# A windowed-attention kernel on one core: transposes in pairs, attention-value beside scores, other places for the convolution, an earlier patch load

## The chip, the core and the metric

The kernel runs on one core of a Trainium2 chip. The time is device time in microseconds (us). "Span" is the time from the first to the last instruction of a profiled execution. TensorE's clock is granted in two steps here, full and half (the 558 clock records of the trace before hold only 1.0 and 0.5), and "clock 0.78" is its mean. Each of these records lasts a multiple of 3.41 us; such a stretch of 3.41 us is called a window. A slot or window is called warm at full clock and cold at half.

## The reference, cut to what matters

```python
# x: (1, 511, 511, 192) bf16; windows of 7 x 7; 4 heads of 48
pe = sum(xp[:, i:i+H, j:j+W, :] * dw_pe[i, j] for i in 0..2 for j in 0..2)   # depthwise 3 x 3
x0 = x + pe
h  = layernorm(x0)                          # over the 192 channels
q, k, v = split(windows(h) @ w_qkv)         # 5329 windows of 49 positions
out = softmax(q @ k.T * 48**-0.5) @ v       # per window and head
return x0 + unwindow(out @ w_o)
```

## The kernel before: the parts that matter

A block is up to 128 windows, one on each partition, and a slot is 8 windows of it: 42 blocks, 667 slots. While the slots of block b do attention, TensorE also does block b+1's convolution (192 small matmuls, slots 0 to 7 of 16), VectorE its statistics (slots 7 to 13), GpSimd its normalisation, and TensorE again its transposes (slots 10 to 15). XP holds the patches that the convolution reads, T its matrix, X the sums x + pe and their normalised form, HO the transposed halves (later also the attention output), and pO a projection that has been copied out. To evict is to copy a result out of PSUM, where the matmuls' results (the tiles ps) lie. Three PSUM tiles of two banks each go round (`PS.next()`), so a stage can start only when the tile used three stages ago has been read.

One transposed group, eight positions, two halves of 96 channels:

```python
def ln_tr(b, s0, n):
    ps = PS.next(); pb = ps[:].bitcast(BF)
    for kt in range(2):
        for i in range(N):                       # 8 transposes into bank kt
            mm(pb[0:KT, kt*1024 + i*128 : ...], lhsT=h[:, s0+i, kt*KT:(kt+1)*KT], rhs=ident[:], is_transpose=True)
        eng = nc.vector.tensor_copy if kt == 0 else nc.scalar.copy
        eng(out=HO[b % 2][0:KT, kt, :, s0:s0+N], in_=pb[0:KT, kt*1024 : ...])
```

One slot, in the order of issue (`hook` issues portions of statistics, loads and stores; `fill` issues the convolutions that are due):

```python
stage_A(b, ck, 0, fill)          # q: 4 matmuls of 392 columns, copied by ScalarE
stage_E(...)                     # attention output transposed back, copied to HO
stage_A(b, ck, 1, fill)          # k
stage_D()                        # attention-value; VectorE: reciprocal, multiply
for s0 in pj: proj(b - 1, s0, fill)   # 8 projection matmuls; ScalarE evicts to pO, GpSimd adds
n.transpose(...)                 # ln_tr, at most one group
stage_B()                        # scores; ScalarE: exp
stage_V(b, ck, fill, ...)        # v: 8 matmuls of 192 columns
```

D and B use TensorE as four tiles of 64 x 64, all else uses the whole array.

## Time and profile before

| | before |
|---|---|
| time, median of 2 | 5380.8 us |
| profiled span | 5361.9 us |
| granted clock | 0.777 |
| before the first slot | 171.1 us |
| mean block (1 to 40) | 124.5 us |

The page lists the busy time of each engine; the list of waits gives, for each row, who waited for whom, the microseconds in total, how often, and the longest one. The prediction below shows the lines. How to read them: TensorE at 83% is not at its limit, as 592 of its some 930 us of idle time are a single wait, and part of its busy time was spent at half clock (0.777 in the mean).

### The profile page before, as it was taken

The page shows a single profiled execution, that of the slowest core. Times are in us where ns is not written, and L with a number is a line of the kernel's source. Part 1 is how long each engine was busy: PE and PEld are TensorE (multiplying, and loading weights), DVE is VectorE, ACT ScalarE, POOL GpSimd, SP SyncE. Part 2 cuts the span into 40 slices and gives each one's busy share as a digit, 9 for nine tenths or more (in the row PEclk, how much of TensorE's full clock was granted, in tenths as well). Part 3 has the DMA queues.
Part 4 walks back from the last instruction along what each step waited for, and adds up shares of the span by engine and source line. Part 5 has one row for each costly group of instructions (what it writes and reads, how often), then busy time and mean ns, then how long its engine had stood idle before and what let it go on. Part 6 is the DMA issues. An engine that isn't in the chain of part 4 may idle for free. (4 is left out here: it accounts for less than half of the span.)

```text
span 5361.9 us, 167300 instructions
## 1 busy us (share of the span) xinstructions
PE 4426.2 (83%) x75049; PEld 3610.8 (67%) x75049; DVE 2727.6 (51%) x4190; ACT 3054.3 (57%) x3855; POOL 2116.4 (39%) x1188
## 2 busy tenths in 40 slices
PE   2688888888888888888888888888888888888777
PEld 1566776776766666677766766666667776676665
DVE  5554555455555544555545555545554555455542
ACT  1455555556555565556655555555555566555555
POOL 3433333334444433334433444433333343344333
PEclk9886787777777776778877777767777888777777
DMA  2222222233333222222323333222222233233221
GB/s 69 59 68 67 68 68 68 68 78 77 82 80 83 72 68 68 68 68 68 78 68 77 83 80 83 71 67 68 68 68 68 68 78 73 70 74 81 68 48 32
DMA packets 529706, 377.00 MB, mean 70 GB/s; under 512 B 454181, under 2 KB 454373, under 8 KB 528979
## 3 DMA queue, kind: packets, MB, share of 16 engines
q1 hardware_dynamic: 528531, 365.92, 27.9%
q8 instruction: 589, 9.65, 0.8%
q14 instruction: 138, 1.13, 0.1%
q10 hardware_dynamic: 448, 0.30, 0.0%
HBM read 265.31 MB, written 100.27 MB: 68 GB/s over the span
## 5 line engine op out<-in xcount | busy, mean ns | idle before, releaser
L467 POOL TENSOR_TENSOR X<-X,pO 128x768 bf16<-128x768 bf16 (+1 forms) x546 | 894.6, 1654 | 2789.2 <-ACT pO L463 2787.9
L364 PE MATMUL ps<-HO,Wqk 96*128 96x392 bf16 x5336 | 1639.4, 426 | 20.1 <-ACT HO L352 15.8
L298 PEld LDWEIGHTS <-XP 81*128 81x128 bf16 x8064 | 1246.8, 185 | 139.2 <-issue 51.6
L298 PE MATMUL psc<-T,XP 81*128 81x49 bf16 x8064 | 1303.1, 211 | 41.3 <-DMA xs<-in_x_dram 32.0
L380 PE MATMUL ps<-Wv,HO 96*128 96x192 bf16 x5336 | 863.4, 299 | 118.3 <-DVE o L433 112.2
L343 PE MATMUL ps<-ident,X 128*96 128x128 bf16 x4116 | 412.0, 253 | 640.9 <-DVE HO L352 592.0
L432 DVE RECIPROCAL rs<-ps 128x16 f32<-128x16 f32 x667 | 169.8, 255 | 1393.8 <-PE ps L423 896.8
L303 DVE CAST X<-psc 128x490 bf16<-128x490 f32 x840 | 542.8, 646 | 591.5 <-PE psc L298 585.0
L364 PEld LDWEIGHTS <-Wqk 96*128 96x128 bf16 x5336 | 623.7, 124 | 303.8 <-issue 238.1
L352 ACT COPY HO<-ps 96x1024 bf16<-96x1024 bf16 (+1 forms) x294 | 284.5, 968 | 869.7 <-PE ps L343 869.7
L343 PEld LDWEIGHTS <-X 128*96 128x96 bf16 x4116 | 336.8, 148 | 644.7 <-issue 598.6
L372 ACT CAST k<-ps 128x784 bf16<-128x784 f32 x667 | 543.6, 815 | 363.8 <-PE ps L364 269.6
L329 POOL TENSOR_TENSOR X<-X,rstd 128x1536 bf16<-128x1536 bf16 (+1 forms) x294 | 734.2, 2515 | 18.5 <-DMA out_dram<-X 5.4
L380 PEld LDWEIGHTS <-HO 96*128 96x128 bf16 x5336 | 604.6, 122 | 158.6 <-issue 111.7
L459 PE MATMUL ps<-Wo,HO 96*128 96x192 bf16 x4116 | 690.6, 302 | 16.3 <-ACT HO L448 12.7
L388 ACT CAST v<-ps 128x768 bf16<-128x768 f32 x667 | 535.7, 803 | 267.3 <-PE ps L380 218.7
L372 ACT CAST q<-ps 128x784 bf16<-128x784 f32 x667 | 543.7, 815 | 249.2 <-PE ps L364 240.9
L433 DVE TENSOR_TENSOR o<-ps,rs 128x768 bf16<-128x768 f32 x667 | 638.4, 957 | 23.4
L459 PEld LDWEIGHTS <-HO 96*128 96x128 bf16 x4116 | 619.1, 180 | 25.2 <-issue 3.5
L463 ACT CAST pO<-ps 128x768 bf16<-128x768 f32 x504 | 401.4, 799 | 392.3 <-PE ps L459 333.4
L447 PEld LDWEIGHTS <-o 128*96 128x96 bf16 x5336 | 526.4, 166 | 104.5 <-issue 45.8
L410 ACT ACTIVATE pt<-ps 128x784 bf16<-128x784 f32 x667 | 550.8, 826 | 62.6 <-PE ps L402 62.5
(55 smaller groups left out, 4068.3 us busy)
## 6 DMA issues: line engine op xcount, KB each, us to landing
XP<-in_x_dram SPq DMA_DIRECT2D x568, 216.0 KB
xs<-in_x_dram SPq DMA_DIRECT2D x574, 168.0 KB
out_dram<-X SPq DMA_DIRECT2D x246, 336.0 KB
XP<-in_x_dram SPq DMA_DIRECT2D x151, 212.6 KB
out_dram<-X SPq DMA_DIRECT2D x82, 168.0 KB
XP<-in_x_dram SPq DMA_DIRECT2D x16, 192.0 KB
XP<-in_x_dram SPq DMA_DIRECT2D x64, 30.4 KB
xs<-in_x_dram SPq DMA_DIRECT2D x63, 23.6 KB
```

The costliest lines, as they stand in the source:

```text
L298: mm(cv.ps[:, (c % 10) * S : (c % 10 + 1) * S], lhsT=XP[0:KP, :, c], rhs=T[0:KP, c, :], start=True, stop=True)
L303: nc.vector.tensor_copy(out=self.X[cv.b % 3][:, :, c0 : c0 + n], in_=cv.ps[:, 0 : n * S].rearrange("p (c s) -> p s c", s=S))
L329: nc.gpsimd.tensor_tensor(out=hbuf(b)[:, s0:s1, :], in0=self.X[b % 3][:, s0:s1, :], in1=rstd[:, i : i + n].unsqueeze(2).to_broadcast([128, ...
L343: mm(pb[0:KT, kt * 1024 + i * 128 : kt * 1024 + (i + 1) * 128], lhsT=h[:, s0 + i, kt * KT : (kt + 1) * KT], rhs=ident[:], start=True, stop ...
L364: mm(ps[:, ab * 512 : ab * 512 + TOK], lhsT=self.Wqk[kt][0:KT, which * 2 + ab, :], rhs=HO[b % 2][0:KT, kt, ck * CH : (ck + 1) * CH, 0:S], ...
L372: nc.scalar.copy(out=dst[:, :, 0:TOK], in_=two_bank(ps, TOK))
L380: mm(ps[:, col : col + C], lhsT=HO[b % 2][0:KT, kt, w : w + 2, :].rearrange("p w s -> p (w s)"), rhs=self.Wv[kt][0:KT, :], start=(kt == 0) ...
L388: eng(out=v_[:].rearrange("p (b j) h e -> p b (j h) e", b=2)[:, :, :, 0:DH], in_=two_bank(ps, 2 * C).rearrange("p b (g d) -> p b g d", d=DH),)
L410: nc.scalar.activation(out=pt[:, 0 : 16 * S].rearrange("p (b n) -> p b n", b=2), in_=two_bank(ps, 8 * S), func=ACTF.Exp, scale=SCALE)
L433: nc.vector.tensor_tensor(out=o_[:].rearrange("p b q (h d) -> p b (q h) d", d=DH), in0=ov[:, :, :, 0:DH], in1=r_[:].rearrange("p (b g) -> ...
L459: mm(ps[:, col : col + C], lhsT=HO[b % 2][0:KT, kt, :, s0 + i], rhs=self.Wo[kt][0:KT, :], start=(kt == 0), stop=(kt == 1))
L467: nc.gpsimd.tensor_tensor(out=xv, in0=xv, in1=o[:, 0:n, :], op=ALU.add)
```

## The change

There are four parts. (a) **Pairs**: both halves of a group are transposed before either is copied. (b) **Order**: attention-value moves behind projection and transposes, next to the scores. (c) **Places**: the convolutions go behind q and k (weight 2) and v (weight 1), no longer behind the projection. (d) **Setup**: the first patch load is issued ahead of the making of the weights, the patch buffer is cleared first and by two engines, and the convolution matrix T is evicted four positions at a time; GpSimd's clearing of X goes behind the matrix that selects for T, which is so ready earlier. The intent is to take the waits and the mode changes (between four tiles and the whole array) off TensorE: in the kernel before, at full clock, 120 ns pass from the start of the last attention-value matmul to the first of the projection (median).

```diff
 def ln_tr(...):                                  # (a)
     for kt in range(2):
         for i in range(N): mm(... is_transpose=True)
+    for kt in range(2):
         eng = nc.vector.tensor_copy if kt == 0 else nc.scalar.copy
...
-            if 0 <= g - LD < NG:                 # (b)
-                stage_D()
             for s0 in pj:
-                proj(b - 1, s0, fill)
+                proj(b - 1, s0)
...
+            if n and g < NG:
+                n.transpose(part(0.56, 0.96, 7), 0.9)
+            if 0 <= g - LD < NG:
+                stage_D()
             if g < NG:
-                if n:
-                    n.transpose(part(0.56, 0.96, 7), 0.9)
                 stage_B()
...
-            nlong = 16 + 8 * len(pj)             # (c)
-            def fill():
-                quota[0] += (conv_goal - conv_start) / nlong
+            def fill(weight):                    # 2 in stage_A, 1 in stage_V
+                quota[0] += (conv_goal - conv_start) * weight / 24
...
+        nc.vector.memset(self.XP[:, 0:88, :], 0.0)     # (d), first of all
+        nc.gpsimd.memset(self.XP[:, 88:BLK, :], 0.0)
-            for n, s0 in enumerate(range(0, S, 2)):    # T: 25 evictions
+            for n, s0 in enumerate(range(0, S, 4)):    # T: 13 evictions
+        for t in self.load_xp(0):                      # ahead of the branch, not behind it
+            t()
```

More of the change, by code (lines that the diff above doesn't have):

```diff
@@ L73, in __init__ @@
         self.PC = _Rot([psum.tile([128, 512], F32, name=f"psc{i}") for i in range(2)])
-        for t in self.PS.t + self.PC.t:
-            nc.vector.memset(t[:], 0.0)
+        self.XP = big.tile([128, BLK, C], BF, name="XP")
+        self.XPr = self.XP[0:KP].rearrange("(r q) n c -> q r n c", q=9)
+        nc.vector.memset(self.XP[:, 0:88, :], 0.0)
+        nc.gpsimd.memset(self.XP[:, 88:BLK, :], 0.0)
         self.ident = consts.tile([128, 128], BF, name="ident")
-        make_identity(nc, self.ident[:])
         self.zero = consts.tile([16, C], BF, name="zero")
         nc.vector.memset(self.zero[:], 0.0)
-        self.XP = big.tile([128, BLK, C], BF, name="XP")
-        self.XPr = self.XP[0:KP].rearrange("(r q) n c -> q r n c", q=9)
         self.T = big.tile([128, C, S], BF, name="T")
@@ L88, in __init__ @@
         gi = consts.tile([1, 1], I32, name="gi")
-        nc.vector.memset(self.XP[:], 0.0)
-        for t in self.X:
-            nc.gpsimd.memset(t[:], 0.0)
         with tc.tile_pool(name="setup", bufs=1) as setup:
@@ L97, in __init__ @@
             for j in range(3):
-                nc.sync.dma_start(out=dwK[9 * j : 9 * j + 3, :], in_=dw_pe[j])
+                nc.scalar.dma_start(out=dwK[9 * j : 9 * j + 3, :], in_=dw_pe[j])
             for kt in range(2):
@@ L115, in __init__ @@
             )
-            for n, s0 in enumerate(range(0, S, 2)):
-                ns = min(2, S - s0)
+            make_identity(nc, self.ident[:])
+            for t in self.PS.t + self.PC.t:
+                nc.vector.memset(t[:], 0.0)
+            for n, s0 in enumerate(range(0, S, 4)):
+                ns = min(4, S - s0)
                 ps = self.PS.next()
@@ L120, in __init__ @@
                     nc.tensor.matmul(
-                        ps[0:KP, ss * C : (ss + 1) * C],
+                        ps[0:KP, (ss // 2) * 512 + (ss % 2) * C : (ss // 2) * 512 + (ss % 2 + 1) * C],
                         lhsT=Sel[0:21, (s0 + ss) * KP : (s0 + ss + 1) * KP],
@@ L126, in __init__ @@
                     )
-                dst = self.T[0:KP, :, s0 : s0 + ns].rearrange("p c s -> p s c")
-                src = ps[0:KP, 0 : ns * C].rearrange("p (s c) -> p s c", c=C)
+                if ns == 4:
+                    dst = self.T[0:KP, :, s0 : s0 + ns].rearrange("p c (b s) -> p c b s", b=2)
+                    src = ps[0:KP].rearrange("p (b n) -> p b n", b=2)[:, :, 0 : 2 * C].rearrange("p b (s c) -> p c b s", c=C)
+                else:
+                    dst = self.T[0:KP, :, s0 : s0 + ns]
+                    src = ps[0:KP, 0 : ns * C].rearrange("p (s c) -> p c s", c=C)
                 (nc.vector.tensor_copy if n % 2 == 0 else nc.scalar.copy)(out=dst, in_=src)
@@ L173, in __init__ @@
             nc.vector.tensor_copy(out=gi[:], in_=gm[:])
+            for t in self.X:
+                nc.gpsimd.memset(t[:], 0.0)
+        for t in self.load_xp(0):
+            t()
         cond = nc.values_load(gi[0:1, 0:1], min_val=0, max_val=1)
@@ L181, in __init__, with dram, clear, load_xp @@
                 self.slow(c2)
+    def dram(self, t, h, w, dims):
+        return bass.AP(tensor=t.tensor, offset=t.offset + (h * self.W + w) * C, ap=[list(d) for d in dims])
+    def clear(self, part, p0, n):
+        nc, zero = self.nc, self.zero[0:9, :]
+        return lambda: nc.sync.dma_start(
+            out=part[:, p0 : p0 + n, :], in_=bass.AP(tensor=zero.tensor, offset=zero.offset, ap=[list(zero.ap[0]), [0, n], [1, C]])
+        )
+    def load_xp(self, b):
+        nc, x, XP, XPr, W, NWR, NWC = self.nc, self.x, self.XP, self.XPr, self.W, self.NWR, self.NWC
+        blocks, clear, dram = _blocks(NWR, NWC), self.clear, self.dram
+        for a0, b0, da, db, n, p0 in blocks[b]:
+            left = [0] if b0 == 0 else []
+            right = [] if b0 + (n - 1) * db < NWC - 1 else list(range(n)) if da else [n - 1]
+            if left and any(ln[1] for bb in blocks[:b] for ln in bb):
+                yield clear(XPr[0], p0, n if da else 1)
+            if right and b:
+                yield clear(XPr[8], p0 + right[0], len(right))
+            last = a0 + (n - 1) * da
+            cuts = [0] + ([1] if da and a0 == 0 else []) + ([n - 1] if da and last == NWR - 1 else []) + [n]
+            for i, j in zip(cuts, cuts[1:]):
+                if j <= i:
+                    continue
+                top, bot = a0 + i * da == 0, a0 + (j - 1) * da == NWR - 1
+                if top and b:
+                    yield clear(XP[0:9], p0 + i, j - i)
+                if bot and b:
+                    yield clear(XP[KP - 9 : KP], p0 + i, j - i)
+                pr0, pr1 = (1 if top else 0), (8 if bot else 9)
+                for pc in range(9):
+                    q, sh = (WS - 1, -1) if pc == 0 else (0, 1) if pc == 8 else (pc - 1, 0)
+                    n0, n1 = i, j
+                    if pc == 0 and left:
+                        n0 = j if da else i + 1
+                    if pc == 8 and right:
+                        n1 = i if da else j - 1
+                    if n1 <= n0:
+                        continue
+                    dims = [[W * C, pr1 - pr0], [WS * C * (W * da + db), n1 - n0], [1, C]]
+                    dst = XPr[pc, pr0:pr1, p0 + n0 : p0 + n1, :]
+                    src = dram(x, WS * (a0 + n0 * da) - 1 + pr0, WS * (b0 + n0 * db + sh) + q, dims)
+                    yield lambda dst=dst, src=src: nc.sync.dma_start(out=dst, in_=src)
@@ L221, in two_bank @@
             return ps[:].rearrange("p (b n) -> p b n", b=2)[:, :, 0:ncol]
-        def dram(t, h, w, dims):
-            return bass.AP(tensor=t.tensor, offset=t.offset + (h * W + w) * C, ap=[list(d) for d in dims])
-        zero = self.zero[0:9, :]
-        def clear(part, p0, n):
-            return lambda: nc.sync.dma_start(
-                out=part[:, p0 : p0 + n, :], in_=bass.AP(tensor=zero.tensor, offset=zero.offset, ap=[list(zero.ap[0]), [0, n], [1, C]])
-            )
-        def load_xp(b):
-            for a0, b0, da, db, n, p0 in blocks[b]:
-                left = [0] if b0 == 0 else []
-                right = [] if b0 + (n - 1) * db < NWC - 1 else list(range(n)) if da else [n - 1]
-                if left and any(ln[1] for bb in blocks[:b] for ln in bb):
-                    yield clear(XPr[0], p0, n if da else 1)
-                if right and b:
-                    yield clear(XPr[8], p0 + right[0], len(right))
-                last = a0 + (n - 1) * da
-                cuts = [0] + ([1] if da and a0 == 0 else []) + ([n - 1] if da and last == NWR - 1 else []) + [n]
-                for i, j in zip(cuts, cuts[1:]):
-                    if j <= i:
-                        continue
-                    top, bot = a0 + i * da == 0, a0 + (j - 1) * da == NWR - 1
-                    if top and b:
-                        yield clear(XP[0:9], p0 + i, j - i)
-                    if bot and b:
-                        yield clear(XP[KP - 9 : KP], p0 + i, j - i)
-                    pr0, pr1 = (1 if top else 0), (8 if bot else 9)
-                    for pc in range(9):
-                        q, sh = (WS - 1, -1) if pc == 0 else (0, 1) if pc == 8 else (pc - 1, 0)
-                        n0, n1 = i, j
-                        if pc == 0 and left:
-                            n0 = j if da else i + 1
-                        if pc == 8 and right:
-                            n1 = i if da else j - 1
-                        if n1 <= n0:
-                            continue
-                        dims = [[W * C, pr1 - pr0], [WS * C * (W * da + db), n1 - n0], [1, C]]
-                        dst = XPr[pc, pr0:pr1, p0 + n0 : p0 + n1, :]
-                        src = dram(x, WS * (a0 + n0 * da) - 1 + pr0, WS * (b0 + n0 * db + sh) + q, dims)
-                        yield lambda dst=dst, src=src: nc.sync.dma_start(out=dst, in_=src)
@@ L269, in strips @@
+        dram, load_xp = self.dram, self.load_xp
         def strips(b, r0, r1):
@@ L370, in stage_A @@
                     )
-                    fill()
+                    fill(2)
             nc.scalar.copy(out=dst[:, :, 0:TOK], in_=two_bank(ps, TOK))
@@ L386, in stage_V @@
                     )
-                    fill()
+                    fill(1)
             eng(
@@ L451, in stage_E, with proj @@
             )
-        def proj(b, s0, fill):
+        def proj(b, s0):
             n = min(4, S - s0)
@@ L459, in proj @@
                     mm(ps[:, col : col + C], lhsT=HO[b % 2][0:KT, kt, :, s0 + i], rhs=self.Wo[kt][0:KT, :], start=(kt == 0), stop=(kt == 1))
-                    fill()
             o = pO.next()
@@ L526, in transpose @@
                 return False
-        xp = list(load_xp(0))
-        for t in xp:
-            t()
         n = Next(0)
@@ L670, in slow @@
         mm = nc.tensor.matmul
+        nc.vector.memset(XP[:], 0.0)
         def two_bank(ps, ncol):
```

## The prediction

> **What bounds the kernel now.** I read the views in this order: the page (which engine is fullest, and at what clock), the list of waits (what TensorE waits for), the timeline of one slot, then stretches of one block. The work is 42 blocks of up to 128 windows. A block is 16 slots of 8 windows (667 slots in all), and all of the next block's convolution, statistics, normalisation and transposes lie inside the slots of the present one.
>
> ```profile
> PE 4426.2 (83%) x75049; PEld 3610.8 (67%) x75049; DVE 2727.6 (51%) x4190; ACT 3054.3 (57%) x3855; POOL 2116.4 (39%) x1188
> PEclk9886787777777776778877777767777888777777
> PE ps L343 <- DVE HO L352: 592.0, 294, 8.8
> PE ps L380 <- DVE o L433: 112.2, 43, 2.8
> ACT pO L465 <- POOL X L467: 60.4, 33, 3.3
> ```
>
> TensorE is the fullest engine, at a granted clock of 0.78, and stands still for some 930 us. Of that, 592 us is one wait, met 294 times (7 a block): the second eight transposes of the layer norm (L343) wait until VectorE has copied the first eight out of PSUM (L352), because both halves are written to one PSUM tile. The timeline shows one of them:
>
> ```profile
> 2627.23 0.44 PE L423 MATMUL ps<-v,pt 49*64 49x49 bf16 x32
> 2627.79 0.26 DVE L432 RECIPROCAL rs<-ps 128x16 f32<-128x16 f32 x1 [4.50 <-PE ps L423]
> 2627.90 0.61 PE L343 MATMUL ps<-ident,X 128*96 128x128 bf16 x8 [0.23 <-ACT HO L448]
> 2628.17 0.96 DVE L433 TENSOR_TENSOR o<-ps,rs 128x768 bf16<-128x768 f32 x1
> 2629.05 1.21 DVE L352 COPY HO<-ps 96x1024 bf16<-96x1024 bf16 x1
> 2630.31 0.61 PE L343 MATMUL ps<-ident,X 128*96 128x128 bf16 x8 [1.81 <-DVE HO L352]
> 2630.85 0.34 PEld L402 LDWEIGHTS <-k 48*64 48x64 bf16 x32
> 2630.96 1.01 ACT L352 COPY HO<-ps 96x1024 bf16<-96x1024 bf16 x1 [2.40 <-PE ps L343]
> ```
>
> The copy is late because the attention-value matmuls (L423) ran just before, so their reciprocal and multiply (0.26 and 0.96) lie ahead of it on VectorE. Three stretches of one block follow, a convolution slot, a transposing slot at half clock and one at full clock (columns: stretch, length, busy time of PE, PEld, DVE, ACT, POOL, granted clock, DMA):
>
> ```profile
> 2411.90:2418.60 6.70, 6.70 (x136) 6.38 (x134) 3.70 (x6) 4.61 (x7) 2.69 (x2) 1.00 0.01 2
> 2492.50:2500.90 8.40, 6.82 (x107) 4.79 (x106) 2.34 (x3) 4.86 (x6) 0.10 (x1) 0.70 0.01 2
> 2625.40:2632.30 6.90, 4.72 (x104) 3.58 (x103) 2.37 (x4) 4.50 (x7) 0.00 (x0) 1.00 0.00 1
> ```
>
> So a convolution slot is bound by TensorE with no gap at full clock; a transposing slot is bound by the wait, and most of them also run at a low clock. I cut the trace at the first q matmul of every slot and averaged blocks 1 to 40, by place in the block (us, granted clock):
>
> ```
> slot   0    1    2    3    4    5    6    7    8    9    10    11    12   13   14   15
> us    8.39 6.64 7.31 6.25 6.85 5.84 6.61 4.46 7.53 7.62 10.03 10.25 9.12 8.71 8.87 10.07
> clock  .53  .76  .90  .91  .97 1.00 1.00 1.00  .94  .61   .74   .67  .68  .68  .70   .68
> ```
>
> The sum is 124.5 us. Slots 10 to 15 hold the transposes and take 57.1 of it. Slot 8 has another gap of 3.0 us (the 112 us row): the burst of statistics on VectorE delays the attention output. Before the first slot lie 171 us of setup:
>
> ```profile
> 24.91 3.40 POOL L106 MEMSET Sel<- 32x3969 bf16 x1
> 59.80 23.48 SPq L267 DMA_DIRECT2D XP<-in_x_dram  x18
> 88.98 17.39 PE L298 MATMUL psc<-T,XP 81*128 81x49 bf16 x192 [32.03 <-DMA xs<-in_x_dram]
> ```
>
> The patches are asked for only at 59.80, after all weights are made, and the convolution starts at 88.98.
>
> [...] its clock records are only 0.5 and 1.0, in multiples of 3.41 us, and a q/k matmul takes 328 ns from start to start at half and 170 at full. I also set each window's busy share beside the next window's clock: a full-clock window under 0.6 busy was nearly always followed by half clock (269 of 270), one over 0.7 never (533 windows), and from half clock it only came back after a window with no gap. [...] from the last tiled attention-value matmul to the first projection matmul is 120 ns at full clock, against some 13 between tiled ones. [...] at full clock a convolution matmul adds 31 ns behind a q/k matmul, 41 behind a v matmul, some 70 behind a projection, but each further one adds 90[...]. [...]
>
> **The change part by part.**
>
> *Pairs.* All 16 transposes, then both copies, VectorE's and ScalarE's. The wait inside the group goes. *Order.* The attention-value matmuls move from ahead of projection and transposes to just ahead of the scores, so VectorE does the HO copy first, then reciprocal and multiply. What takes the place of the old wait is found from the rotation of three PSUM tiles: v takes the transposes' tile (free when both copies end) and the next q takes the attention-value tile (free when the multiply ends). At full clock, from the end of the transposes: VectorE's copy starts at 0.1 and its successor 1.1 later, the multiply starts 0.3 after that and takes 0.96, plus 0.1: 2.55 us to the next q. From that q to the end of the transposes: q 0.72, E 0.70, k 0.68 (four times 170), 16 transposes at 66 ns with drain 1.15: 3.2. A cycle is 5.75 to 5.9 us where it was 6.9 warm and 8.4 to 9 mostly cold. In the 2.55 us TensorE has attention-value 0.45, scores 0.45 and v 0.7, so about 0.95 us of gap is left, in two pieces. That is 72% busy in the worst 3.4 us window: above the cooling limit. At half clock the same work takes 2.65 us, there is no gap, and the clock can rise. So I expect slots 13 and 14 warm at 5.9. ScalarE needs 4.5 us a slot and does not bind. Slots 10 to 12 also carry the statistics: VectorE work from the table of items is about 5.3, 8.1 and 4.1 us, and part of the windows will be cold; I take 7.0, 6.8 and 6.5, plus 1.0 in slot 10 for the wait of the last projection's eviction on GpSimd (L465 above), which was hidden and no longer is. Slot 15 has the short seventh group and its data wait: 7.1. Sum 40.2 instead of 57.1: 16.9 a block.
>
> *Neighbours.* Attention-value beside scores saves two changes of tiling mode, some 0.2 us, in slots with a projection. *Convolution beside q, k, v only.* A slot with 16 projection matmuls had 27 convolutions on 32 places: 6.75 x 31 + 6.75 x 41 + 13.5 x 72 = 1.46 us. Now 18 behind 8 q/k and 9 behind 8 v: 8 x 31 + 10 x 90 + 8 x 41 + 90 = 1.57. With 8 projections 1.48 becomes 1.61; with none it stays 1.61. So this part costs 0.1 and the neighbours return 0.2: slots 3 to 6 give 0.4 together. Slots 7 to 9: from 19.6 to 18.5, as slot 8's gap moves from v to the next q, behind 0.8 us more of TensorE work and one more statistics item (3.0 to about 2.5), and its cooling stays. Slots 0 to 2: from 22.3 to 21.0; the end of slot 15 still has some 2 us of gaps within one window (waits for copy, multiply and the seventh group), so slot 0 still starts cold. A block gains 16.9 + 1.1 + 1.3 + 0.4 = 19.7 us; 667/16 = 41.7 blocks: 821 us.
>
> *Setup.* XP is cleared first, by two engines (88 of 128 columns: 7.1 us of the 10.3), so the 18 loads of 23.5 us start near 9 instead of 60 and lie beside the weights. The 25 evictions of T (2.06 and 1.94 us, alternating, 22 us) become 13 of twice the size that write runs of four elements: I take about 11 us. Selection is ready near 15 (was 32.4), the branch near 32, VectorE's clearing before its first eviction 10 more, so the convolution runs at about 44 to 62 rather than 89 to 107: 45 us, and 3 from the seven transposes ahead of the loop. Sum 48.
>
> 5381 - 821 - 48 = 4512; with rounding towards a clock somewhat better than assumed in slots 0 to 2, 4490.
>
> **The rivals.** *VectorE takes the wait's place and the clock stays low.* For: VectorE's chain is my limit in every transposing slot, and rising needs a window with no gap at all. An all-cold slot is 8 x 328 ns + E 1.15 + transposes 2.0 + 0.7 + 0.7 + v 1.25 = 8.4 us, so slots 10 to 15 would fall only to about 51.5 and the total to about 4980. Against: cold there is no gap. *The whole block warms.* If slots 10 to 12 reach 5.9 and slot 0 starts warm, another 3.1 + 2.3 us a block go: about 4270. For: one 2611 to 2632 stretch stayed at full clock even with the old wait. *Only the wait goes, with nothing behind it and no change of clock*: 592 + 48 gives 4740. *GpSimd or DMA becomes the bound.* GpSimd's slots 8 to 12 hold some 33 us, and it was busy 10.32 of 10.40 us in one slot; the block's transfers must fit into 54 rather than 77 us of slots 7 to 15, at shares up to 0.76 already. Either would add 2 to 5 us a block: 4590 to 4720. *The change does nothing*: it would need TensorE's wait to return whole on v and q; the arithmetic above leaves 0.95 of 1.8.
>
> **Range and chances.** The terms differ mostly in one thing, the clock of slots 8 to 15 and 0 to 2; between the warm rival and a mixture of the cold and the GpSimd ones lies 4260 to 4850. A return of all of 870 us is far off, so faster 0.98.
>
> **What would show it.** The row of L343 waiting for VectorE's HO falls from 592 to under 100 us; new rows of v (L380's successor) waiting for HO and of q waiting for o, some 0.4 us each; the granted clock rises to between 0.83 and 0.92; transposing slots without statistics last 5.7 to 6.1 us; patch loads start near 9 us and the first slot near 123. Wrong it would be if those slots stayed over 7.5 us, if the clock stayed under 0.8, or if q and v wait over 1.5 us a slot.

## The result, and the profile after

The changed kernel takes 4787.7 us (median of 2, 4765.7 to 4809.8), 0.890 of the time before (interval 0.872 to 0.908). The ratios are not quite the ratios of the medians. Run again later beside others it was 0.894 (0.890 to 0.898). The prediction was 4490 us, 4260 to 4850: inside the range, on its slow side.

From the page of the changed kernel:

```profile
PE 3856.7 (81%) x75049; PEld 3329.1 (70%) x75049; DVE 2714.9 (57%) x4184; ACT 3032.9 (64%) x3849; POOL 2103.3 (44%) x1189
...
PEclk9888888888888888888888888888888888878788
```

TensorE was busy for 570 us less with the same 75049 matmuls, which goes with the clock, 0.875 instead of 0.777. Its waits, from the list of waits (L353, L363, L375, L391, L413, L434, L444, L473, L475 and L477 are what were L343, L352, L364, L380, L402, L423, L433, L463, L465 and L467):

```profile
PE ps L391 <- ACT HO L363: 391.4, 246, 6.2
...
ACT HO L363 <- DVE HO L363: 310.8, 212, 5.6
...
ACT pO L475 <- POOL X L477: 135.3, 41, 5.0
...
PE ps L413 <- ACT pO L475: 116.6, 40, 4.3
...
PE ps L391 <- ACT pO L473: 91.5, 323, 1.1
...
PE ps L375 <- DVE o L444: 75.8, 44, 1.9
```

The 592 us row is gone. In its place v (L391) waits 1.6 us, 246 times, for ScalarE's copy of the transposes, and that copy waits for VectorE's. The timeline of one transposing slot at nearly full clock shows it (start, duration, engine, line; in brackets the idle time before it and what ended it):

```profile
2402.80 1.05 PE L353 MATMUL ps<-ident,X 128*96 128x128 bf16 x16
...
2403.79 0.44 PE L434 MATMUL ps<-v,pt 49*64 49x49 bf16 x32
2403.96 1.22 DVE L363 COPY HO<-ps 96x1024 bf16<-96x1024 bf16 x1 [3.11 <-PE ps L353]
...
2404.23 0.44 PE L413 MATMUL ps<-q,k 48*64 48x49 bf16 x32
...
2405.22 1.01 ACT L363 COPY HO<-ps 96x1024 bf16<-96x1024 bf16 x1 [1.04 <-DVE HO L363]
2405.38 0.96 DVE L444 TENSOR_TENSOR o<-ps,rs 128x768 bf16<-128x768 f32 x1
...
2406.28 1.04 PE L391 MATMUL ps<-Wv,HO 96*128 96x192 bf16 x8 [1.60 <-ACT HO L363]
```

VectorE's copy ends at 2405.18 and ScalarE's starts at 2405.22, although ScalarE had been idle for 1.04 us. The setup did what it was to do:

```profile
9.75 22.01 SPq L234 DMA_DIRECT2D XP<-in_x_dram  x18
...
15.01 23.69 POOL L178 MEMSET X<- 128x9408 bf16 x3
...
30.90 0.14 DVE L175 CAST gi<-gm 1x1 int32<-1x1 f32 x1
...
60.27 22.11 SPq L234 DMA_DIRECT2D XP<-in_x_dram  x18
```

The second row of loads starts when the convolution of block 0 is done: at 60.27 now, at 106.41 before.

Cut by slots as in the prediction (mean of blocks 1 to 40, us and granted clock; "gap" is TensorE's idle time, counted with the slot of the matmul that ends it, so the wait of slot 9's first q stands in slot 9 though it lengthens slot 8):

```
slot            0    1    2    3    4    5    6    7    8    9   10   11   12   13   14   15   sum
before us     8.39 6.64 7.31 6.25 6.85 5.84 6.61 4.46 7.53 7.62 10.03 10.25 9.12 8.71 8.87 10.07 124.5
after us      8.04 6.18 6.87 6.00 6.66 6.04 6.66 4.45 6.57 6.89 9.20 8.14 7.55 6.43 7.50 7.80 111.0
after clock    .65  .86  .96  .99 1.00 1.00 1.00 1.00  .98  .75  .89  .73  .80  .93  .79  .88
after gap     1.88  .45  .28  .32  .28  .30  .27  .27  .40 2.12 3.97 1.85 1.93 1.66 1.74 1.73
```

So the span lost 598 us: 49 ahead of the first slot (171.1 to 122.3) and 549 behind it.

### The profile page after: what moved, and what is told of

The parts are those of the page before. It is cut to its first block, busy times and chain, and to the rows that moved or that the text cites. A ratio compares the mean times of both kernels' runs of the same rounds, so it can differ in the third digit from the quotient of the medians.

```text
span 4764.0 us, 167034 instructions
## 1 busy us (share of the span) xinstructions
PE 3856.7 (81%) x75049; PEld 3329.1 (70%) x75049; DVE 2714.9 (57%) x4184; ACT 3032.9 (64%) x3849; POOL 2103.3 (44%) x1189
## 4 chain that ended last, share of the span: by engine, by line
PE 55%; ACT 13%; DVE 12%; POOL 9%; issue 4%; SPq 4%; DMA 3%; ACTq 0%; DVEq 0%; POOLq 0%
PE ps L375 19%; PE ps L391 11%; PE psc L308 9%; PE ps L458 7%; ACT pO L473 6%; POOL X L339 5%; DVE HO L363 5%; ACT HO L363 5%; PE ps L353 4%; PE ps L470 4%; SPq L234 3%; DVE bnst L324 3%; DVE X L320 3%; POOL X L477 2%; POOL rstd L331 2%
## 5 line engine op out<-in xcount | busy, mean ns | idle before, releaser
L477 POOL TENSOR_TENSOR X<-X,pO 128x768 bf16<-128x768 bf16 (+1 forms) x546 | 869.6, 1608 | 2295.5 <-ACT pO L473 2293.9
L375 PE MATMUL ps<-HO,Wqk 96*128 96x392 bf16 x5336 | 1614.6, 393 | 113.8 <-DVE o L444 75.8
L308 PEld LDWEIGHTS <-XP 81*128 81x128 bf16 x8064 | 1099.3, 177 | 167.2 <-issue 109.8
L308 PE MATMUL psc<-T,XP 81*128 81x49 bf16 x8064 | 1076.7, 221 | 42.7 <-DMA XP<-in_x_dram 33.7
L391 PE MATMUL ps<-Wv,HO 96*128 96x192 bf16 x5336 | 707.9, 264 | 483.0 <-ACT HO L363 391.4
L375 PEld LDWEIGHTS <-Wqk 96*128 96x128 bf16 x5336 | 650.9, 126 | 318.2 <-issue 205.6
L391 PEld LDWEIGHTS <-HO 96*128 96x128 bf16 x5336 | 549.4, 108 | 447.2 <-issue 416.9
L363 DVE COPY HO<-ps 96x1024 bf16<-96x1024 bf16 (+1 forms) x294 | 337.0, 1147 | 761.9 <-ACT k L383 399.8
L444 DVE TENSOR_TENSOR o<-ps,rs 128x768 bf16<-128x768 f32 x667 | 638.7, 958 | 23.3
L458 PEld LDWEIGHTS <-o 128*96 128x96 bf16 x5336 | 490.3, 155 | 82.3 <-issue 32.4
L363 ACT COPY HO<-ps 96x1024 bf16<-96x1024 bf16 (+1 forms) x294 | 284.5, 968 | 393.7 <-DVE HO L363 310.8
L324 DVE BATCH_NORM_STATS2 bnst<-X 128x6 f32<-128x384 bf16 x1050 | 527.7, 549 | 10.1
L458 PE MATMUL ps<-ident,o 128*96 128x128 bf16 x5336 | 520.7, 254 | 1.4 <-DVE o L444 1.4
L470 PE MATMUL ps<-Wo,HO 96*128 96x192 bf16 x4116 | 463.9, 263 | 4.1 <-ACT pO L473 3.0
L470 PEld LDWEIGHTS <-HO 96*128 96x128 bf16 x4116 | 444.3, 183 | 28.1 <-issue 16.6
```

The source lines that it names most:

```text
L308: mm(cv.ps[:, (c % 10) * S : (c % 10 + 1) * S], lhsT=XP[0:KP, :, c], rhs=T[0:KP, c, :], start=True, stop=True)
L324: nc.vector.bn_stats(out=bnst[:, i, :], in_=self.X[b % 3][:, s : s + 2, :].rearrange("p s c -> p c s"))
L363: eng(out=HO[b % 2][0:KT, kt, :, s0 : s0 + N], in_=pb[0:KT, kt * 1024 : kt * 1024 + N * 128].rearrange("p (s w) -> p w s", w=128),)
L375: mm(ps[:, ab * 512 : ab * 512 + TOK], lhsT=self.Wqk[kt][0:KT, which * 2 + ab, :], rhs=HO[b % 2][0:KT, kt, ck * CH : (ck + 1) * CH, 0:S], ...
L391: mm(ps[:, col : col + C], lhsT=HO[b % 2][0:KT, kt, w : w + 2, :].rearrange("p w s -> p (w s)"), rhs=self.Wv[kt][0:KT, :], start=(kt == 0) ...
L444: nc.vector.tensor_tensor(out=o_[:].rearrange("p b q (h d) -> p b (q h) d", d=DH), in0=ov[:, :, :, 0:DH], in1=r_[:].rearrange("p (b g) -> ...
```

## The experiments

Twelve kernels ran, in three sets of four (e1 to e4, e5 to e8, e9 to e12), each set beside the kernel before on one chip. All were correct.

| run | kernel | median us | ratio to before | interval |
|---|---|---|---|---|
| e1 | before + pairs | 4957.4 | 0.921 | 0.916 to 0.925 |
| e2 | before + order | 4937.9 | 0.916 | 0.912 to 0.920 |
| e3 | before + places | 5456.6 | 1.013 | 1.008 to 1.018 |
| e4 | before + setup | 5335.2 | 0.991 | 0.984 to 0.998 |
| e5 | changed + two PSUM tiles | 4600.9 | 0.860 | 0.854 to 0.865 |
| e6 | changed + own buffer | 4796.6 | 0.896 | 0.890 to 0.901 |
| e7 | changed, old places | 4805.7 | 0.898 | 0.892 to 0.903 |
| e8 | changed + all three | 4521.5 | 0.846 | 0.840 to 0.851 |
| e9 | changed, again | 4788.9 | 0.894 | 0.890 to 0.898 |
| e10 | before + pairs + order | 4853.3 | 0.906 | 0.902 to 0.910 |
| e11 | changed + two tiles + own buffer | 4659.0 | 0.867 | 0.862 to 0.872 |
| e12 | e8, statistics late | 4511.4 | 0.842 | 0.838 to 0.845 |

### One part at a time: e1 to e4, e10

The edits of e1 to e4 are the parts (a) to (d) of the diff above, each alone in the kernel before.

> The kernel before with the pairs alone: all 16 transposes ahead of both copies; attention-value stays ahead of projection and transposes. Theory A (the gain of the block comes from the wait inside the group): the 592 us wait goes, and a new one comes at the next q, which needs both copies, made one after the other behind reciprocal and multiply. A warm transposing slot without statistics then lasts about 6.2 us where it was 6.9; span about 4960 us, ratio 0.92, granted clock 0.85. Theory B (the gain comes from VectorE's shorter chain, that is from the new order): pairs alone only move the wait from the transposes to q, and the ratio is 0.97 or more.

Measured 0.921: theory A's figure. But the waits of e1 say how much is left, and by whom:

```profile
ACT HO L353 <- DVE HO L353: 547.8, 250, 6.0
...
PE ps L365 <- ACT HO L353: 280.0, 240, 2.3
...
PE ps L381 <- DVE o L434: 123.2, 59, 3.2
```

The transposes' 592 us are gone, and q (L365) now waits 1.2 us, 240 times, for ScalarE's copy: 280 us come back. A warm slot 13 or 14 lasts 6.33 us (6.2 expected). The gaps are shorter, and the clock is 0.843 instead of 0.777.

> The kernel before with the new order alone: attention-value just ahead of the scores, behind projection and transposes; the second half of each transposed group still waits for VectorE's copy. Theory A: that wait shrinks from 592 us to about 380 (1.3 us each, since the copy is no longer behind reciprocal and multiply), v then waits about 1 us for ScalarE's copy; ratio about 0.97. Theory B: most of the block's gain is here, ratio 0.93 or less. On both, slot 8 loses its 2.8 us wait of v for the multiply, and the slots with a projection save 0.2 us of mode changes, unless v waits there for the projection's eviction instead.

Measured 0.916: here theory B's figure, though e1 had given A's.

```profile
PE ps L343 <- DVE HO L352: 501.9, 294, 8.8
...
PE ps L380 <- ACT HO L352: 84.3, 187, 0.5
...
PE ps L364 <- DVE o L433: 77.1, 47, 1.9
```

The wait inside the group is still 502 us, 90 less than before (slots 13 and 14: 1.4 us where it was 1.7 and 1.9), and still the order alone gains 449 us. Slots 8 and 9 take 13.3 us instead of 15.2, as v no longer waits 2.8 us for the multiply and q of slot 9 waits 1.8. Slots 13 to 15 take 22.4 instead of 27.6, slots 0 to 3 27.4 instead of 28.6, and the mean clock is 0.857: more than the shorter waits themselves. So neither theory is right alone: each of the two parts shortens the gaps, and with either the clock rises.

> The kernel before with pairs and order together, old setup, old convolution places. If the two parts remove the same wait in two ways (each alone gave 8%), together they give little more than one alone: 0.90 to 0.91. If they were independent they would give 0.844. The setup part (0.009) on top of it is the changed kernel with the old convolution places.

Measured 0.906 where independence would give 0.844 (0.921 x 0.916): the two parts are two ways to most of the same gain. Slots 10 to 15 take 45.6 us in e1, 49.5 in e2 and 47.3 in e10: added to the pairs, the order makes the transposing slots no shorter. What e10 gains on e1 lies in slots 0 to 2 (24.1 to 21.7) and 7 to 9 (19.5 to 17.6).

> The kernel before with the convolution behind q, k and v alone. As the prediction reckons it from the cost of a convolution behind each kind of matmul: 0.1 us longer in five slots of a block, 5 to 6 us... that is 0.6 us a block, 25 us in all: ratio 1.005. The rival[...] has it faster by 1% or more.

Measured 1.013: slower, by 70 us, near three times the term. The mean slots say where. Slots 4 to 6, at full clock or nearly, take 19.47 us against 19.30, which is 0.06 us a slot and less than the predicted 0.1. Slots 0 to 3 take 30.28 us against 28.59, at a clock of 0.50, 0.65, 0.80 and 0.86 where it was 0.53, 0.76, 0.90 and 0.91. So the direct cost was sized right and the rest is a clock that comes back later.

> The kernel before with the early patch load and the faster making of T alone: 45 to 50 us less ahead of the first slot, blocks unchanged: span about 5313 us, ratio 0.991. If the four parts add up, the four differences sum to 598 us of span; if they need one another, e1 and e2 together fall short of the 550 us that the blocks gained.

Measured 0.991, span 5319.6 us: as expected. The four differences sum to 429 + 449 - 70 + 52 = 860 us, far over the 598 of the change, so the parts don't add up; pairs and order overlap.

### Why the two copies are one after the other: e5

```diff
-            ps = PS.next()
-            pb = ps[:].bitcast(BF)
             for kt in range(2):
+                pb = PS.next()[:].bitcast(BF); pbs.append(pb)
                 for i in range(N):
-                    mm(pb[0:KT, kt*1024 + i*128 : ...], ...)
+                    mm(pb[0:KT, i*128 : ...], ...)
             for kt in range(2):
-                eng(out=HO[...], in_=pb[0:KT, kt*1024 : ...])
+                eng(out=HO[...], in_=pbs[kt][0:KT, 0 : ...])
```

> The changed kernel, with the two halves of a transposed group in two PSUM tiles of the same rotation. Theory A (ScalarE's copy waits for VectorE's because both read one PSUM tile): the 311 us for which ScalarE's HO waits for VectorE's HO go, v's 391 us of waiting for it fall below 100, slots 13 and 14 last about 5.4 us, as the prediction had meant them with both copies side by side, and the clock there is 0.95 or more; the kernel gains 200 to 250 us on the changed one: about 4540 us, 0.844 of the kernel before. Theory B (they wait because both write one HO tile, or because ScalarE is still busy with k): the row stays near 311 us and the time within 1% of the changed kernel's, about 0.89.

Measured 0.860, some 190 us faster than the changed kernel (4600.9 us against 4788.9 in e9, of another set): theory A, a little short of the 200 to 250 us that it gave. The same stretch of a slot in e5:

```profile
2319.11 1.31 PE L354 MATMUL ps<-ident,X 128*96 128x128 bf16 x16
...
2319.82 1.22 DVE L364 COPY HO<-ps 96x1024 bf16<-96x1024 bf16 x1 [2.11 <-ACT HO L460]
...
2320.45 1.01 ACT L364 COPY HO<-ps 96x1024 bf16<-96x1024 bf16 x1
2320.51 0.44 PE L435 MATMUL ps<-v,pt 49*64 49x49 bf16 x32
...
2321.10 0.44 PE L414 MATMUL ps<-q,k 48*64 48x49 bf16 x32
...
2321.51 0.82 PE L392 MATMUL ps<-Wv,HO 96*128 96x192 bf16 x8
```

The copies overlap, at unchanged durations of 1.22 and 1.01 us, which the prediction had assumed and the trace before could not show. And v starts 1.1 us after the end of the transposes, where it was 2.4. No row "ScalarE's HO for VectorE's HO" is left among the 60 longest waits, and v waits 3.2 us in all for HO. Both copies still write one HO tile, so that rival is out. It is the program's own order: in the changed kernel's list of instructions ScalarE's copy waits on VectorE's semaphore alone (250 of 252 copies), in e5 on TensorE's alone (245 of 252). Two tiles also let VectorE start half a group earlier; the run doesn't separate that from the overlap. They also change the rotation: the scores now take the tile of VectorE's half and wait for its copy, most of all in slot 12 (2.3 us), where that copy lies behind the statistics:

```profile
PE ps L414 <- DVE HO L364: 147.2, 110, 5.1
```

Slots 13 to 15 fall from 6.43, 7.50 and 7.80 us to 5.81, 5.08 and 6.13. Slots 10 and 12 stay at 9.23 and 7.18, and slots 0 to 2 get longer, 23.1 instead of 21.1 us. In slot 0 the convolution now waits 1.4 us for the DMA of the patches (0.7 in the changed kernel, 0.2 before).

### What holds slot 10: e6

```diff
+        pO1 = pool.tile([128, 1, C], BF, name="pO_one")
-            o = pO.next()
+            o = pO.next() if n == 4 else pO1      # the last projection has one position
```

> The changed kernel, with a buffer of its own for the last projection of a block (one position instead of four), so that ScalarE's eviction need not wait for GpSimd's addition two projections back. If that wait sets slot 10: ScalarE's 135 us and the 117 us of the scores behind it go, slot 10 falls from 9.2 to about 6.5 us, and the kernel gains 100 to 120 us: about 4660, 0.866 of the kernel before. If slot 10 is held by VectorE's statistics in any case, v or q waits instead and the gain is under 40 us.

Measured 0.896: no gain. In e6 the waits for GpSimd at this place are gone from the list, and another has grown by what they were:

```profile
PE ps L392 <- ACT HO L364: 525.9, 246, 8.8
ACT HO L364 <- DVE HO L364: 455.6, 250, 8.6
```

v waits 526 us instead of 391 (in slot 10 by 3.9 us in the mean, where it was 0.6). In slot 10 VectorE's copy lies behind the statistics, so a TensorE freed from GpSimd runs into that. The second alternative holds.

### The places of the convolution once more: e7, e8, e11

e7 is the changed kernel with part (c) taken back. e8 has that, e5's and e6's edits; e11 has e5's and e6's alone.

> The changed kernel with the convolution's old places (behind q, k, v and projection alike). By the prediction's term, 0.6 us a block, it gains 25 us (0.885); by what the convolution part did alone (1.3% slower, nearly all in slots 0 to 3 at a lower clock), 50 to 70 us (0.877). If the places pay only together with the new order, as the change intends, it loses instead (0.895 or more).

Measured 0.898 against 0.896 of e6 in the same set: no difference, so neither gain came; the loss that the third alternative expects cannot be told from noise. Slots 3 and 5 are shorter by 0.23 and 0.10 us, but slots 0 to 2 take 22.3 us instead of 21.1.

> The changed kernel with two tiles and the last projection's own buffer, the convolution left in its new places (behind q, k, v); against the earlier run with all three it tells what the convolution's places do. By the prediction's term 25 us slower than with the old places (0.851), by the part alone in the old kernel 50 to 70 us slower (0.858); if the places don't matter, 0.845.

Measured 0.867 against e8's 0.846 (of another set): here the new places cost 2.5%, much more than any of the three figures. Slots 0 to 3 of e11 take 30.7 us (clock .61, .61, .76, .89), those of e8 26.1 (.91, .92, .97, 1.00), while slots 4 to 6 are 19.5 and 19.4. So the places act through the clock at the start of a block (e3, e11), or not measurably (e7). Beside e5 (0.860), e11 shows once more that the last projection's own buffer gains nothing.

> The changed kernel with all three: two tiles, the last projection's own buffer, the old places. If the three add up: 230 + 110 + 40 us less than the changed kernel, about 4400 us, 0.818 of the kernel before. If GpSimd or VectorE's statistics in slots 8 to 12 take over as the bound, no more than the two tiles alone gain, about 0.84.

Measured 0.846: less than the sum, as slots 9, 10 and 12 stay at 7.8, 9.0 and 8.2 us. It is some 5.4% faster than the changed kernel by the two ratios. What it gains on e5 lies in slots 0 to 2, 20.3 us against 23.1, again at a higher clock.

### Whether the order on VectorE holds slots 8 to 12: e9, e12

> The changed kernel itself, unchanged, as the yardstick of this set: 0.885 to 0.898 of the kernel before, as first measured (0.890) and as its variants of the last set suggest.

Measured 0.894, as said above. The second run of this set starts from e8:

```diff
-                    n.stats(int(s_start + (s_goal - s_start) * share))
+                    n.stats(int(s_start + (s_goal - s_start) * max(0.0, 2 * share - 1)))
```

> The kernel with all three (two tiles, own buffer, old places), and the statistics of a slot issued only behind the scores, not in five portions through the slot, so that VectorE's copy of the transposes, the reciprocal and the multiply are never behind them. If slots 8 to 12 are held by the order on VectorE, they fall from 38 to about 33 us and the kernel to about 4330 us (0.81). If VectorE's (or GpSimd's) amount of work in those slots holds them, the wait moves to the next slot and the time stays within 1% of 0.846.

Measured 0.842: within 1% of e8, and the intervals overlap. Slots 8 and 9 did fall, from 6.58 and 7.81 us to 5.07 and 5.29, but slot 10 rose from 9.03 to 11.78 us. The waits of e12:

```profile
PE ps L355 <- POOL X L340: 261.2, 48, 37.0
...
PE ps L415 <- DVE HO L365: 188.1, 126, 15.6
```

and three stretches, slots 8, 9 and 10 of one block (busy of PE, PEld, DVE, ACT, POOL, then clock and DMA):

```profile
2221.95:2227.02 5.07, 4.35 (x99) 3.49 (x97) 4.88 (x9) 4.73 (x7) 2.00 (x2) 1.00 0.29 83
2227.02:2232.31 5.29, 4.92 (x105) 4.24 (x105) 4.42 (x9) 4.92 (x7) 2.47 (x3) 1.00 0.76 176
2232.31:2244.05 11.74, 6.45 (x109) 5.48 (x108) 5.93 (x11) 5.01 (x8) 10.60 (x6) 0.77 0.85 210
```

TensorE waits 5.3 us in slot 10 for GpSimd's normalisation, and GpSimd is busy 10.60 of 11.74 us. Slot 12 still waits 3.8 us for VectorE's copy behind the statistics (3.1 in e8). What VectorE no longer holds up in slots 8 and 9, GpSimd does in slot 10. So moving work within VectorE's order does not shorten the chain of statistics, normalisation and transposes as a whole. As the edit itself makes the statistics later, the run does not show how far GpSimd alone would hold these slots.

## Why the prediction was right, and where it was off

The predicted and measured terms of a block (us, rounded, so that sums can be off by 0.1):

| slots | before | predicted | after | e5 |
|---|---|---|---|---|
| 0 to 2 | 22.3 | 21.0 | 21.1 | 23.1 |
| 3 to 6 | 25.6 | 25.2 | 25.4 | 25.7 |
| 7 to 9 | 19.6 | 18.5 | 17.9 | 18.2 |
| 10 to 15 | 57.0 | 40.2 | 46.6 | 40.4 |
| sum | 124.5 | 104.8 | 111.0 | 107.4 |

- **The mechanism held.** The wait inside the group went whole, a part returned through the rotation of PSUM tiles, and the clock rose into the stated range: 0.875 of 0.83 to 0.92. What still holds slots 10 and 12 in e8 and e12 is VectorE's copy behind the statistics and GpSimd's normalisation, near what the GpSimd rival named.
- **That the total fell in the range is partly luck.** The blocks gave 549 us of the 821 predicted: slots 10 to 15 fell short by 6.4 us a block, while slots 7 to 9 gave 0.6 more than predicted. The slow side of the range stood for a mixture of the cold and the GpSimd rivals. Slots 11, 12 and 14 were indeed cold in part, but no rival names what made them so, two copies in sequence.
- **Setup: 48 predicted, 49 measured.** Loads from 9.75 us (near 9), the branch behind 30.90 (near 32), the evictions of T 10.6 us in all (about 11; they take 1.10 us each, where those of half the size took 2.06 and 1.94), the end of block 0's convolution at 60 (62), the first slot at 122.3 (123).
- **The mis-sized term is "All 16 transposes, then both copies" and the cycle of 5.75 to 5.9 us that rests on it.** It took VectorE's and ScalarE's copies to run side by side, with 0.95 us of gap left in two pieces of about 0.45, at v and at the next q. They run one after the other, so v waits 1.66 to 1.92 us a slot in slots 11 to 15, and q hardly at all outside slot 9. A warm slot is little longer for it: slot 13 took 6.0 us in the 23 of 40 blocks in which its clock was over 0.97, within the 5.7 to 6.1 predicted. The loss comes through the clock. A gap of 1.73 us in one piece leaves a window of 3.41 us about half busy, where the prediction reckoned 72% and no cooling; after full-clock windows under 60% busy the clock fell 222 times of 263, after those over 70% 6 times of 707. So the means of slots 13 and 14 were 6.43 and 7.50 us. One of the prediction's own signs of error, over 1.5 us of waiting at v, did appear, and slot 14 stands at the limit of another (7.5 us). That this is the term is shown by e5: with the copies side by side the gaps of slots 13 to 15 fall to 0.3 us and less, and slots 10 to 15 take 40.4 us against 40.2 predicted. That the sums agree so well is luck, as slot 10 is longer (9.2 against 8.0) and slot 14 shorter (5.1 against 5.9) than reckoned. The warning stood in the profile before: transposes into one bank waited for a read of the other (the row of 592 us), so the program was ordering by whole tiles.
- **Slot 10: "plus 1.0 for the wait of the last projection's eviction" was 2.9 us** at the scores. But e6 shows that this wait covers another of the same size, VectorE's copy behind the statistics, so 7.0 for the slot was too low whatever GpSimd does.
- **Neighbours and places: 0.4 us predicted for slots 3 to 6, 0.2 measured.** At full clock (medians, from start to start), the steps from k to attention-value, projection and scores took 261, 120 and 183 ns; those from k to projection, attention-value and scores now take 172, 182 and 25. That is 0.19 us less where 0.2 was predicted, so the mode changes did go. But v took the place of attention-value in the rotation and waits 0.27 to 0.32 us in those slots for ScalarE's eviction of the projection (the row of 91.5 us). The direct cost of the places was about right (0.06 us a slot in e3); the delay of the clock that they can bring, 1.3% in e3, was not foreseen.
- **Slot 8: 2.5 us of gap predicted at the next q, 1.8 us measured**, in slot 9.
- **Slips that decide nothing.** The 54 us that the DMA rival gives slots 7 to 15 do not follow from the prediction's terms (18.5 + 40.2 = 58.7); they took 64.5. The "some 13" ns between tiled matmuls are the length of a stage over its 32 matmuls; from start to start the mean is 8 ns at full clock. The 1.15 us for "16 transposes at 66 ns" are an estimate: at full clock they start 56 ns apart (median), and attention-value starts 149 ns after the last of them, 0.99 us in all in the slot shown above.

When the clock falls, both traces show: half clock followed 269 of 270 full-clock windows under 60% busy and none of 533 over 70% before, 222 of 263 and 6 of 707 after. What stays open is when it comes back. Among half-clock windows at least 99% busy in slots 0 to 3, the next window was at full clock in 43% before, 30% in e3, 28% in e5 and e11, 65% in e8, 59% in e7, 90% in e2 and 75% in e10, but 67% in the changed kernel, which has the new places too. So in two of the three pairs that differ by the places alone (e3 against before, e11 against e8) the new places go with a later full clock, in the third (the changed kernel against e7) they don't, and no run here tells why. Nor does the prediction's reading hold that the clock rises only after a window with no gap: it did in the trace before (all 278 rises), but in the changed kernel 28 of 228 rises followed windows that were 93 to 99% busy.

The fastest kernels, e8 and e12, beat the changed kernel too: 0.846 and 0.842.

## What to carry to other kernels

When a wait inside a stage is removed, follow the buffer's next user: ask which instructions must finish before the tile comes free, and whether they can really run at the same time, which needs separate tiles if the program orders by tiles, as here (0.860 with two tiles against 0.894). Where the clock follows the gaps, as here, two remedies for the same gap need not add up (0.921 and 0.916 alone, 0.906 together, where 0.844 would be their product), and a small change elsewhere can cost more through the clock than by its own work (e3: 70 us, where 25 were reckoned). Test the parts singly: here one of the four (the places) lost time or gained nothing clear of noise wherever it was tried.
